# Row transfers released from the transposition, a first input loaded in halves, a convolution moved: one Trainium2 kernel of convolution, Fourier transform and MLP

## The chip, the core and the metric

The kernel runs on one core of a Trainium2 chip. The core has five instruction streams that run side by side and meet at semaphores: TensorE (PE; its weight loads are shown apart as PEld), VectorE (DVE), ScalarE (ACT), GpSimd (POOL) and SyncE (SP), which here only issues DMA transfers. The 16 DMA engines move data between DRAM and the on-chip memory. The metric is the device time of one execution in microseconds (us); less is better. A program's framework (a tile scheduler) puts the instructions of each stream in an order when the kernel is built, and adds the semaphore waits; on the chip each stream runs in that order and waits where it must.

## What is computed

Input `x` is (8, 4224, 192): eight batches of 4224 tokens. First a convolution along the tokens with seven taps per head, the taps a softmax of the weights; then the real part of a 2-D Fourier transform over tokens and channels is added; then a layer norm and an MLP (192 to 768 to 192, ReLU), with a residual.

```python
w = np.exp(weight - np.max(weight, axis=-1, keepdims=True))
w = w / (np.sum(w, axis=-1, keepdims=True) + 1e-09)
x_pad = np.concatenate([np.zeros((B, K - 1, D)), x], axis=1)
x_unf = x_pad[:, idx, :].reshape(B, S, K, H, D // H)
x = np.einsum('hk,bskhg->bshg', w, x_unf).reshape(B, S, D)
...
X = np.fft.fft(np.fft.fft(x, axis=1), axis=2)
u = x + np.real(X)
un = (u - mean(u)) / np.sqrt(var(u) + 1e-06)
out = u + np.maximum(un @ w_ch1, 0.0) @ w_ch2
```

## The kernel before

**Stages of a batch.** (1) *Convolution* (`conv_unit`, L397): windows `xt` of the input meet a banded matrix on PE (L417, PSUM tile `pc`), ACT or DVE evict them into `xa` (L423, L426), ACT sums their squares (L367), and `store_rows` (L372) writes the rows into a scratch `sc` in DRAM. (2) *Load and split*: the rows come back as `xs` with the token index as 33a + 128b (a on the partitions, 33 values of b in eight pieces), and `split_x` (L517) makes two fp16 parts, XH on ACT (L527) and XL on DVE (L528). (3) `stage_a` (L534): the transform over a, 16 tiles `pa`, evicted into the halves `yh` and `yl` (L553, L554). It reads all b at once, so it needs all eight pieces. (4) `stage_b` (L559): the transform over b and part of the channels, PSUM tile `pb`, evicted into V (L580, L582). (5) For each of the nine steps of a batch: `load_res` (L597) brings the convolved rows of that step from the scratch into the tile `u`; `prep` (L645) does the last transform on PE (L669, PSUM tile `pq`), adds it to `u` on DVE (L686, "the sums"), takes mean and variance (L693, L694), normalises on POOL into `un` and splits into `hl` (L722 to L739); `transposes` (L749) turns `hl` into `kt` by a DMA transposition on SP's queue; `mlp_hidden` (L767, PSUM tile `ph`) makes `hh` on ACT and its low part `hlo` on DVE (L786, L787); `mlp_out` (L791, PSUM tile `po`) adds its result into `u` (L813) and stores `u` (L821).

**Rows of a step.** `u` has four groups of rows. Groups 0 and 2 come by ordinary transfers on SP's queue (two or three each, L612); groups 1 and 3 by one indirect DMA each, which POOL issues (L618). There are eight `u` tiles; a step uses the tile that the step eight before it has left, so its transfers wait until that step's output store has landed.

**Order.** The loop at L997 runs over the 72 steps. At step n it places the MLP of step n, `prep` of steps n+2 and n+3, the transposition of step n+2, the rows of step n+4, and the stages 1 to 4 of later batches. `tc.issue_after(x)` makes the scheduler issue an instruction behind x. Before, the ordinary row transfers of all but the first four steps were so held behind `turn[0]`, the transposition that was placed last; the indirect ones behind `lows`, the last POOL instruction of `hl` two or three steps earlier. SP's transfers use eight semaphores in turn: one is issued only when the eighth before it has landed.

**The start.** Batch 0's convolution runs first, without cover. `load_first_x` (L491) loads its scratch back in 16 transfers: four ranges of b by four ranges of a, sorted by the last row that each reads. The ranges with b under 17 go to a tile in the space of `yh`, the others to one in that of `yl` (they read `xs_yh` and `xs_yl` in the profile). From L976 on, written by hand: the second transform's first tile, the convolution of the second batch in chunks (`conv_chunk`, L969; its matmuls held behind `staged["pe"]`), and the first `prep`, `sums` being its four pieces up to the norm's factor and `rest` the last two.

Of the kernel before, what the change touches and what calls it, by code (L numbers as in the profile page):

```python
# [34 lines left out]
AC = 32  # L35
# [91 lines left out]
def kernel(  # L127
# [363 lines left out]
    def load_first_x(bt):  # L491

        halves = [
            sb.tile([NA, 17, D], F32, tag=tag, name=f"xs_0_{tag}", bufs=1)
            for tag in ("yh", "yl")
        ]

        def rows_of(b0, b1):
            h, o = (halves[0], 0) if b0 < 17 else (halves[1], 17)
            return h[:, b0 - o : b1 - o]  # L500

        loads = []
        for b0, b1 in ((0, 9), (9, 17), (17, 25), (25, 33)):
            for ch in range(NA // AC):
                r = 33 * AC * ch + 128 * b0 - (S if b0 >= WRAP[ch] else 0)
                loads.append((r + 33 * (AC - 1) + 128 * (b1 - 1 - b0), r, ch, b0, b1))
        for _, r, ch, b0, b1 in sorted(loads):
            src = bass.AP(
                bt.sc.tensor, bt.sc.offset + r * D,
                [[33 * D, AC], [128 * D, b1 - b0], [1, D]],  # L510
            )
            load = nc.sync.dma_start(rows_of(b0, b1)[AC * ch : AC * (ch + 1)], src)
        for i, piece in enumerate(PIECES):
            bt.xs[i] = rows_of(*piece)
        return load.ins
# [43 lines left out]
    def stage_b(bt, it):  # L559
# [3 lines left out]
        for h in range(CG // CT):  # L563
            pb = ps.tile([128, CT, 2 * NM], F32, tag="f", name=f"pb_{b}_{it}_{h}", bufs=4)
            for i in range(CT):
                c = it * CG + h * CT + i

                parts = ((0, 2, NM),) if c else ((0, 1, NM), (1, 2, 0))
                for e0, e1, at in parts:
                    for n, (y, l) in enumerate(((bt.yh, 0), (bt.yh, 1), (bt.yl, 0))):  # L570
                        mm = nc.tensor.matmul(  # L571
                            pb[NJ * e0 : NJ * e1, i],
                            y[:NBD, c, e0:e1].rearrange("p e j -> p (e j)"),
                            R[:, l, at : at + 2 * NM],
                            start=(n == 0), stop=(n == 2),
                        )
# [7 lines left out]
                )  # L584

        if b + it == 0:
            staged.update(pe=mm.ins, act=up.ins)
        if it == 0:
            bt.V0 = sb.tile([128, 2, 6, 64], F16, tag="V0", name=f"V0_{b}")
        nc.gpsimd.tensor_copy(  # L590
# [6 lines left out]
    def load_res(bt, it, g):  # L597
# [6 lines left out]
        def fetch(part, first, *dims):  # L604
            src = bass.AP(
                bt.sc.tensor,
                bt.sc.offset + first * D,
                [[step * D, n] for step, n in dims] + [[1, D]],
            )
            late = turn[0] if b * NIT + it > 3 else None  # L610
            with tc.issue_after(late) if late else ExitStack():
                nc.sync.dma_start(part, src)  # L612

        if it == Q0 or g % 2:
            col = 0 if it == Q0 else 1 + 4 * it + g
            k = b * NIT + it
            with after(lows.get(k - 2, lows.get(k - 3))):
                nc.gpsimd.indirect_dma_start(  # L618
                    to, None, bt.sc[:S],
                    bass.IndirectOffsetOnAxis(ap=rows_sb[:, col : col + 1], axis=0),  # L620
                )
            return
# [22 lines left out]
    def prep(bt, it):  # L645
# [16 lines left out]
        for at, t in rows:  # L662
            for k3 in range(ND):

                po = pq[at, k3, 0] if it == Q0 else pq[at, k3]
                for r in range(2):
                    for n, (v, l) in enumerate(((0, 0), (0, 1), (1, 0))):
                        rhs = G[:, l, r, k3, t]
                        nc.tensor.matmul(  # L669
                            po, weights(v, ND * r + k3),  # L670
                            rhs[:, 0] if it == Q0 else rhs,
                            start=(r + n == 0), stop=(r == 1 and n == 2),
                        )

        uf = u.rearrange("p g (c k) -> p g c k", k=ND)
        pt = pq.rearrange("p k t c -> p t c k")
        if it == Q0:
# [296 lines left out]
            )  # L974

    stage_b(first, 0)  # L976
    conv_chunk(0)
    for f in sums(0) + rest(0):
        f()
    transposes(first, 0)  # L980
    conv_chunk(1)
# [110 lines left out]
```

## Time and profile before

| | us |
|---|---|
| median of three runs | 1274.29 (1269.73 to 1274.59) |
| the profiled execution | 1266.11 |
| its span, first to last instruction | 1264.1 |
| TensorE busy in it | 1175.6 (93%) |
| VectorE, GpSimd, ScalarE busy | 819.6, 769.2, 599.8 |
| DMA moved | 170.47 MB, mean 135 GB/s |

All rows shown below are of that profiled execution, in us from the start of its span. A row of the timeline has start, length, engine (SPq: SP's queue), line, operation and tiles written and read, a count, and in brackets how long the engine stood before it and what ended that. A busy TensorE is not TensorE at its peak, since the ends of its matmuls are modelled.

### The profile page before, as it was taken

What the parts mean: (1) busy time and instruction counts of PE and PEld (TensorE: products, weight loads), DVE (VectorE), ACT (ScalarE), POOL (GpSimd) and SP (SyncE); (2) the same over time, 40 slices, a digit from 0 to 9 for tenths busy, and PEclk for the clock granted to TensorE, in tenths of its full rate; (3) what the DMA queues carried; (4) which work ended last, traced back from release to release, by engine and by line L of the source; (5) the groups of instructions that cost most, each with busy time, mean ns of one, the idle gap of its engine ahead of it and who ended that gap; (6) DMA issues with size and microseconds to landing.
All of it is one profiled execution on the core that took longest, in us unless ns stands there. A gap on an engine that the chain in (4) does not pass through costs nothing.

```text
span 1264.1 us, 30150 instructions
## 1 busy us (share of the span) xinstructions
PE 1175.6 (93%) x12224; PEld 931.5 (74%) x12224; DVE 819.6 (65%) x1871; ACT 599.8 (47%) x983; POOL 769.2 (61%) x1103
## 2 busy tenths in 40 slices
PE   4089889998999999999899999999899999999998
PEld 4078667786778777887677867778677877777766
DVE  6666485677646865476655876467965687566543
ACT  4556564365444555446444554446444454332222
POOL 0206776577646777468564786557774778757760
PEclk9589999999999999999999999999999999999999
DMA  8933784558554675477654677555754444322331
GB/s 300 264 103 102 223 204 121 134 137 156 130 121 122 174 153 143 93 166 173 113 135 115 136 178 142 126 128 129 181 120 114 121 126 96 79 61 67 94 73 41
DMA packets 238506, 170.47 MB, mean 135 GB/s; under 512 B 119512, under 2 KB 222112, under 8 KB 238368
## 3 DMA queue, kind: packets, MB, share of 16 engines
q1 hardware_dynamic: 193912, 130.75, 43.3%
q10 hardware_dynamic: 37928, 24.44, 7.4%
q0 software_dynamic: 6528, 13.38, 4.5%
q8 instruction: 95, 1.56, 0.5%
q14 instruction: 43, 0.35, 0.1%
HBM read 83.82 MB, written 58.55 MB: 113 GB/s over the span
## 4 chain that ended last, share of the span: by engine, by line
PE 64%; DVE 10%; POOL 8%; DMA 8%; issue 3%; SPq 3%; ACT 2%; ACTq 0%; DVEq 0%; POOLq 0%
PE ph L782 24%; PE po L801 8%; PE po L807 8%; PE po L804 8%; DMA u<-sc 4%; PE pc L417 4%; PE pb L571 4%; PE pa L545 4%; PE pq L669 4%; POOL hl L739 2%; DVE u L686 2%; POOL u L618 2%; POOL y L714 2%; POOL un L722 2%; DVE hlo L787 2%
## 5 line engine op out<-in xcount | busy, mean ns | idle before, releaser
L782 PE MATMUL ph<-kt,W 128*128 128x512 f16 (+1 forms) x2160 | 493.0, 361 | 18.7 <-DVE hlo L787 17.5
L786 ACT ACTIVATE hh<-ph 128x512 f16<-128x512 f32 (+1 forms) x400 | 236.9, 592 | 443.9 <-PE ph L782 412.5
L787 DVE SCALAR_TENSOR_TENSOR hlo<-ph,hh 128x512 f16<-128x512 f32 (+1 forms) x400 | 270.9, 679 | 269.7 <-ACT hh L786 261.6
L801 PE MATMUL po<-W,hh 128*128 128x192 f16 x1584 | 386.3, 247 | 3.6 <-DVE u L813 2.8
L807 PE MATMUL po<-W,hlo 128*128 128x192 f16 x1584 | 387.0, 247 | 1.5 <-DVE hlo L787 1.5
L804 PE MATMUL po<-W,hh 128*128 128x192 f16 x1584 | 386.2, 247 | 0.0
L782 PEld LDWEIGHTS <-W 128*128 128x128 f16 x2160 | 192.1, 97 | 161.5 <-issue 16.0
L722 POOL TENSOR_SCALAR un<-u,mv,y 128x192 f32<-128x192 f32 x260 | 268.8, 1039 | 7.9
L618 POOL DMA_INDIRECT u<-sc,rows_sb x136 | 152.4, 1121 | 67.7 <-DMA xs_yl<-sc 36.8
L807 PEld LDWEIGHTS <-hlo 128*128 128x128 f16 x1584 | 155.2, 98 | 23.6 <-DVE hlo L787 1.9
L801 PEld LDWEIGHTS <-hh 128*128 128x128 f16 x1584 | 155.6, 98 | 19.4 <-ACT hh L786 1.6
L804 PEld LDWEIGHTS <-hh 128*128 128x128 f16 x1584 | 155.2, 98 | 17.6 <-issue 3.4
L686 DVE SCALAR_TENSOR_TENSOR u<-pq,g,u 128x128 f32<-128x128 f32 (+1 forms) x328 | 104.8, 379 | 69.5 <-DMA u<-sc 52.9
L545 PE MATMUL pa<-c_sb,XH 128*128 128x128 f16 x1024 | 101.4, 222 | 32.3 <-DMA xt<-in_xw_dram 24.9
L417 PE MATMUL pc<-xt,band 128*120 128x144 f32 x724 | 114.8, 297 | 15.0 <-DMA band<-line_d 11.0
L713 POOL TENSOR_SCALAR v<-mv 128x4 f32<-128x4 f32 (+1 forms) x71 | 17.1, 241 | 177.6 <-DVE mv L694 154.1
L739 POOL TENSOR_TENSOR hl<-un,hl 128x512 f16<-128x512 f32 (+2 forms) x142 | 119.5, 862 | 3.5
L590 POOL COPY V<-V 128x96 f16<-128x96 f16 x64 | 16.4, 260 | 172.9 <-DVE V L582 171.5
L417 PEld LDWEIGHTS pc<-xt,band 128*120 128x120 f32 x724 | 100.5, 189 | 23.5 <-issue 10.9
L545 PEld LDWEIGHTS <-XH 128*128 128x128 f16 x1024 | 81.9, 98 | 42.7 <-ACT XH L527 26.4
L553 ACT ACTIVATE yh<-pa 99x512 f16<-99x512 f32 x128 | 76.2, 597 | 77.5 <-PE pa L545 71.7
L528 DVE SCALAR_TENSOR_TENSOR XL<-xs,s_x,XH 128x768 f16<-128x768 f32 (+1 forms) x56 | 92.5, 1653 | 17.3 <-ACT XH L527 17.2
(132 smaller groups left out, 1570.4 us busy)
## 6 DMA issues: line engine op xcount, KB each, us to landing
out_dram<-u SPq DMA_DIRECT2D x64, 384.0 KB
xt<-in_xw_dram SPq DMA_DIRECT2D x40, 576.0 KB
sc<-xa ACTq DMA_DIRECT2D x30, 540.0 KB
xs<-sc SPq DMA_DIRECT2D x28, 288.0 KB
u<-sc SPq DMA_DIRECT2D x72, 96.0 KB
sc<-xa SPq DMA_DIRECT2D x12, 540.0 KB
xs<-sc SPq DMA_DIRECT2D x28, 192.0 KB
xs<-sc SPq DMA_DIRECT2D x7, 480.0 KB
```

The costliest lines, as they stand in the source:

```text
L417: nc.tensor.matmul(pc[:WR, h - h0], band[:, h, :WR], xt[:, :, h * GRP : (h + 1) * GRP], start=True, stop=True,)
L545: nc.tensor.matmul(pa[:, i], x[:, at], F[:, l], start=(n == 0), stop=(n == 2))
L618: nc.gpsimd.indirect_dma_start(to, None, bt.sc[:S], bass.IndirectOffsetOnAxis(ap=rows_sb[:, col : col + 1], axis=0),)
L686: nc.vector.scalar_tensor_tensor(to, src, bt.g, to, op0=ALU.mult, op1=ALU.add)
L722: (nc.vector if b + it == 0 else nc.gpsimd).tensor_scalar(un[:, g], u[:, g], mv[:, g, 0:1], y[:, g : g + 1], op0=ALU.subtract, op1=ALU.mult,)
L739: lower = (nc.vector if b + it == 0 else nc.gpsimd).tensor_tensor(bl[:, :, o : o + n], un[:, :ng, f], hi[:, :, f], op=ALU.subtract)
L782: nc.tensor.matmul(ph[:, n], W1[:, w, ht * 128 : (ht + 1) * 128], kt[:, k], start=(i == 0), stop=(i == len(order) - 1),)
L786: anchor[0] = nc.scalar.activation(hh, ph, AF.Relu).ins
L787: nc.vector.scalar_tensor_tensor(hlo, ph, 0.0, hh, op0=ALU.max, op1=ALU.subtract)
L801: nc.tensor.matmul(po[:, g % 2], hh[:, ht, tk], W2[:, ht, 0], start=(ht == 0), stop=False)
L804: nc.tensor.matmul(po[:, g % 2], hh[:, ht, tk], W2[:, ht, 1], start=False, stop=False)
L807: nc.tensor.matmul(po[:, g % 2], hlo[:, ht, tk], W2[:, ht, 0], start=False, stop=(ht == 5),)
```

## The change

Three parts. The row transfers (L612) are no longer held behind a transposition, and the indirect ones (L618) are held behind `lows` in the first batch alone. The first input's sixteen loads are sorted by half of b first (those under 17, then the others). And `sums(0)`, the first `prep` up to its norm, is written ahead of the second batch's first convolution chunk, whose matmuls are now held behind the last matmul of the first sums instead of the second transform's first tile.

```diff
@@ load_first_x
-                loads.append((r + 33 * (AC - 1) + 128 * (b1 - 1 - b0), r, ch, b0, b1))
-        for _, r, ch, b0, b1 in sorted(loads):
+                last = r + 33 * (AC - 1) + 128 * (b1 - 1 - b0)
+                loads.append((b0 >= 17, last, r, ch, b0, b1))
+        for _, _, r, ch, b0, b1 in sorted(loads):
@@ stage_b
-            staged.update(pe=mm.ins, act=up.ins)
+            staged.update(act=up.ins)
@@ load_res
-            late = turn[0] if b * NIT + it > 3 else None
-            with tc.issue_after(late) if late else ExitStack():
-                nc.sync.dma_start(part, src)
+            nc.sync.dma_start(part, src)
...
-            with after(lows.get(k - 2, lows.get(k - 3))):
+            with after(lows.get(k - 2, lows.get(k - 3)) if k < NIT else None):
@@ prep
+        staged.setdefault("pe", mm.ins)
@@ the start
     stage_b(first, 0)
+    for f in sums(0):
+        f()
     conv_chunk(0)
-    for f in sums(0) + rest(0):
+    for f in rest(0):
         f()
```

What the scheduler makes of it, at three places. First, SP's queue at the sixteen loads of the first input, before (xs_yh is the half with b under 17; 32x8 or 32x9 are rows of a by values of b):

```order
L512 DMA xs_yl<-sc_130 32x8x192 x2
L512 DMA xs_yh<-sc_130 32x8x192
L512 DMA xs_yh<-sc_130 32x9x192
L512 DMA xs_yl<-sc_130 32x8x192 x2
L512 DMA xs_yh<-sc_130 32x8x192
L512 DMA xs_yh<-sc_130 32x9x192
L512 DMA xs_yl<-sc_130 32x8x192 x2
L512 DMA xs_yh<-sc_130 32x8x192
L512 DMA xs_yh<-sc_130 32x9x192
```

(two of `xs_yl` and two of `xs_yh` follow once more), and in the change:

```order
L513 DMA xs_yh<-sc_130 32x8x192
L513 DMA xs_yh<-sc_130 32x9x192
L513 DMA xs_yl<-sc_130 32x8x192 x2
L513 DMA xs_yh<-sc_130 32x8x192
L513 DMA xs_yh<-sc_130 32x9x192
L513 DMA xs_yl<-sc_130 32x8x192
L513 DMA xs_yh<-sc_130 32x8x192
L513 DMA xs_yh<-sc_130 32x9x192
L513 DMA xs_yh<-sc_130 32x8x192
L513 DMA xs_yh<-sc_130 32x9x192
L513 DMA xs_yl<-sc_130 32x8x192 x5
```

The eight loads of `xs_yh` are now among the first eleven, where they were spread over all sixteen. On ACT and DVE the pieces of `xs_yh` are split first, where those of `xs_yl` were; the first two pieces that ACT takes are those of the 32x8 loads.

Second, PE at the first sums. Before, behind the second transform's first tile (pc is the second batch's convolution, pq the sums' PSUM tile, V_0 the weights of its matmuls):

```order
L417 MATMUL pc_0_0_697<-xt_0_632,band 120x144 x3
L417 MATMUL pc_0_3_702<-xt_0_632,band 120x144 x3
L417 MATMUL pc_0_6_707<-xt_0_632,band 120x144 x2
L417 MATMUL pc_1_0_771<-xt_1_634,band 120x144 x3
L669 LDWEIGHTS V_0_659
L669 MATMUL pq_0_716<-c_sb,V_0_659 128x130
```

and in the change:

```order
L668 LDWEIGHTS V_0_659
L668 MATMUL pq_0_695<-c_sb,V_0_659 128x130
L417 MATMUL pc_0_0_740<-xt_0_632,band 120x144 x3
L417 MATMUL pc_0_3_745<-xt_0_632,band 120x144 x3
L417 MATMUL pc_0_6_750<-xt_0_632,band 120x144 x2
L417 MATMUL pc_1_0_771<-xt_1_634,band 120x144 x3
```

All eighteen `pq` matmuls are now ahead of the convolution. Behind the first two of them, which need V's high half alone, 24 matmuls of the second transform's next tile stand, where six stood before.

Third, SP's queue in the third batch's third and fourth step (u_4 is the tile of that batch's step 4, counted from 0; kt_2 the transposition of step 2; xs and xt are inputs of the next two batches; out_dram an output store), before:

```order
L753 DMA_TRANSPOSE kt_2_5847<-hl_2_5766 128x12x128
L612 DMA u_4_5770<-sc_1462 80x1x192
L612 DMA u_4_5770<-sc_1462 48x1x192
L354 DMA xt_1_5903<-in_xw_dram 128x1152
L612 DMA u_5_5975<-sc_1462 128x1x192
L487 DMA xs_7_6012<-sc_3781 32x4x192
L487 DMA xs_7_6012<-sc_3781 96x4x192
L821 DMA out_dram<-u_0_4763 128x768
L753 DMA_TRANSPOSE kt_3_6034<-hl_3_5971 128x12x128
L612 DMA u_5_5975<-sc_1462 96x1x192
L612 DMA u_5_5975<-sc_1462 32x1x192
```

and in the change:

```order
L611 DMA u_6_6197<-sc_1462 128x1x192
L611 DMA u_6_6197<-sc_1462 112x1x192
L611 DMA u_6_6197<-sc_1462 16x1x192
L611 DMA u_7_6439<-sc_1462 128x1x192 x2
L487 DMA xs_6_5977<-sc_3781 32x4x192
L487 DMA xs_6_5977<-sc_3781 96x4x192
L487 DMA xs_7_6012<-sc_3781 32x4x192
L487 DMA xs_7_6012<-sc_3781 96x4x192
L753 DMA_TRANSPOSE kt_2_5847<-hl_2_5766 128x12x128
L354 DMA xt_1_5903<-in_xw_dram 128x1152
L821 DMA out_dram<-u_0_4763 128x768
L753 DMA_TRANSPOSE kt_3_6034<-hl_3_5971 128x12x128
```

The rows of steps 4 and 5 stood behind the transpositions of steps 2 and 3; now those of steps 6 and 7 stand ahead of the transposition of step 2, and so do both `xs` loads. POOL's indirect transfers move by as much. At the start, likewise, the eleven transfers for the first batch's steps 4 to 7 stand ahead of the second batch's first store and of the first transposition, directly behind seven for steps 0, 2 and 3. On DVE the parts of a step's sums, which stood apart where a part of the rows came later, now stand together; the number of evictions and splits between them is the same.

More of the change, by code (lines that the diff above doesn't have):

```diff
@@ L570, in stage_b @@
                     for n, (y, l) in enumerate(((bt.yh, 0), (bt.yh, 1), (bt.yl, 0))):
-                        mm = nc.tensor.matmul(
+                        nc.tensor.matmul(
                             pb[NJ * e0 : NJ * e1, i],
@@ L668, in prep @@
                         rhs = G[:, l, r, k3, t]
-                        nc.tensor.matmul(
+                        mm = nc.tensor.matmul(
                             po, weights(v, ND * r + k3),
```

## The prediction

> **What bounds the kernel now.** I read the page first, for the span and the slices, then the busy time by stretches, then who waited for whom on the two engines that matter, TensorE (PE) and VectorE (DVE), and last the timeline at the places the change touches.
>
> ```profile
> span 1264.1 us, 30150 instructions
> PE   4089889998999999999899999999899999999998
> ```
>
> Each digit is a slice of 31.6 us. TensorE is full except in the first slices, the second of them empty, so the matmuls set the time, and time can be won only where TensorE stands. There are two such places. The first is the start, here by stretches of 20 us (busy time of PE, PE's weight loads, DVE, ACT, POOL; then granted clock, DMA share, GB/s):
>
> ```profile
> 40.00:60.00 20.00, 0.00 (x0) 0.00 (x0) 9.10 (x8) 10.21 (x9) 4.04 (x5) 0.50 1.10 251
> 140.00:160.00 20.00, 15.42 (x131) 11.54 (x131) 11.75 (x21) 13.95 (x19) 16.30 (x18) 1.00 0.90 258
> ```
>
> From 40 to 60 us nothing runs on PE while the DMA engines are full: the first batch's convolved rows come back from DRAM. From 140 to 160 us PE lacks 4.6 us. The second place is the steady part, where each batch takes nine steps:
>
> ```profile
> 200.00:250.00 50.00, 50.00 (x516) 38.99 (x515) 26.45 (x67) 20.79 (x41) 27.46 (x47) 1.00 0.58 139
> 250.00:300.00 50.00, 47.59 (x513) 38.09 (x511) 37.56 (x79) 29.00 (x40) 38.39 (x51) 1.00 0.66 159
> ...
> 1000.00:1050.00 50.00, 49.85 (x533) 39.00 (x531) 40.16 (x90) 26.60 (x35) 40.59 (x55) 1.00 0.44 112
> ```
>
> Most stretches are full; one or two in each batch lack 2 us and more. The waits of PE and of DVE from 200 us to the end (total, times, longest) say why:
>
> ```profile
> PE ph L782 <- DVE hlo L787: 16.4, 21, 2.3
> PE pa L545 <- DVE u L686: 4.6, 3, 1.8
> ```
>
> ```profile
> DVE u L686 <- DMA u<-sc: 46.0, 15, 5.7
> ```
>
> PE stands 21.0 us because DVE is late with the low half of the hidden layer or stands itself at the sums of L686; and DVE stands 46.0 us in 15 places because the rows `u`, which SP fetches from the scratch, are not there. That is the wait the change aims at. One such place, first SP's issues, then DVE:
>
> ```profile
> 278.03 2.02 SPq L753 DMA_TRANSPOSE kt<-hl  x1
> 280.10 1.62 SPq L612 DMA_DIRECT2D u<-sc  x2
> ```
>
> ```profile
> 283.80 1.24 DVE L686 SCALAR_TENSOR_TENSOR u<-pq,g,u 128x192 f32<-128x192 f32 x4 [3.73 <-DMA u<-sc]
> ```
>
> The two row transfers start the moment the transposition in front of them is issued, and DVE, idle for 3.73 us, goes on 2 us after them. DVE executes in order, so the next eviction of the hidden layer waits too.
>
> **The change part by part.**
>
> *The split input of the first transform.* The first stage needs all of XH and XL, so all eight pieces must be split (ACT, then DVE) before PE starts. SP's rows, then ACT, DVE and PE:
>
> ```profile
> 46.05 0.38 SPq L954 DMA_DIRECT2D taps<-line_d  x1
> 48.41 2.90 SPq L354 DMA_DIRECT2D xt<-in_xw_dram  x2
> ```
>
> ```profile
> 53.35 0.87 SPq L612 DMA_DIRECT2D u<-sc  x1
> ```
>
> ```profile
> 50.83 6.11 ACT L527 ACTIVATE XH<-xs_yl,s_x 128x768 f16<-128x768 f32 x4 [9.79 <-DMA xs_yl<-sc]
> 56.84 6.55 ACT L527 ACTIVATE XH<-xs_yh,s_x 128x768 f16<-128x768 f32 x4
> 63.42 1.85 DVE L528 SCALAR_TENSOR_TENSOR XL<-xs_yh,s_x,XH 128x960 f16<-128x960 f32 x1 [0.30 <-ACT XH L527]
> 65.33 0.29 PE L545 MATMUL pa<-c_sb,XL 128*128 128x128 f16 x1 [0.85 <-DVE XL L528]
> ```
>
> SP issues a transfer only when the eighth before it has landed, so its issues tell landings. Counting the 16 loads as 1 to 16, `taps` is number 18 and waits for load 10 (landed by 46.05 at the latest), `xt` is 19 (load 11 by 48.41), the third row transfer is 23 (load 15 by 53.35). Now: the first `yl` pieces need load 13, and ACT starts at 50.83. Changed: the order shows all eight loads of the half `yh` among the first eleven, and the two pieces that ACT takes first need only numbers 1, 5, 8, 10. So ACT starts at 46.1, the four `yh` pieces (6.55 us) end at 52.7, with load 11 in time for the third. The `yl` pieces then wait for load 15 until 53.4, and end 6.1 us later at 59.5. DVE follows with the last piece, which is now a `yl` one of 1.5 us in place of the 1.85 us: 61.1. PE passes its wait at 61.2 in place of 65.33: **4.1 us**. The bounds: 2.4 us, if load 11 counts for all four pieces (48.41 against 50.83), and 4.7 us (46.1 against 50.83). Matmuls and bytes stay the same.
>
> What the clock does to this stage:
>
> ```profile
> 66.00:68.00 2.00, 2.00 (x22) 2.00 (x20) 0.69 (x1) 0.91 (x2) 0.00 (x0) 0.50 0.96 238
> ...
> 70.00:72.00 2.00, 2.00 (x39) 2.00 (x37) 2.00 (x4) 1.75 (x4) 0.00 (x0) 1.00 0.17 49
> ```
>
> After the idle stretch PE runs at 0.50 for some 5 us; a tile of twelve matmuls takes 1.1 us there and 0.6 us later, where DVE (about 0.7 us a tile) is the slower. Earlier or later release therefore moves the stage's end by some 0.4 us per us. [...]
>
> *The second batch's convolution behind the first sums.* The chain of waits and DVE:
>
> ```profile
> 78.75 1.30 PE pb L571 x23
> 80.05 2.75 PE pc L417 x22
> ...
> 83.19 0.92 PE pq L669 x16
> ```
>
> ```profile
> 80.17 1.07 DVE L582 SCALAR_TENSOR_TENSOR V<-pb,V 128x408 f16<-128x408 f32 x2 [1.48 <-ACT V L580]
> ```
>
> The sixteen `pq` matmuls need DVE's V, done at 81.24, but stand behind convolution matmuls until 83.19. In the changed order 24 matmuls of the second transform's next tile stand there, 1.1 us, which end before 81.24. The sums start 83.19 - 81.24 = **1.9 us** earlier, and with them the first normalisation and transposition. The moved convolution runs while DVE and ACT normalise, where PE stood anyway. Bounds: nothing, if ACT's evictions of the moved chunk come before the square root that it also does for the norm, and 2.75 us.
>
> *Row transfers not held.* At the start SP now issues eleven more transfers ahead of the second batch's first store and the first transposition:
>
> ```profile
> 63.90 6.58 SPq L612 DMA_DIRECT2D u<-sc  x7
> 82.54 1.15 SPq L381 DMA_DIRECT2D sc<-xa  x2
> ```
>
> Seven took 6.58 us, so eleven end 10.3 us after 70.5, at 80.8, and the store behind them, due 0.6 us earlier than now, at 81.9. It is hidden, with 1.1 us to spare; the transposition comes 3.6 us later still. If that cover goes, each us is lost in full.
>
> In the stretch from 140 to 160 us the row transfers for steps 4 and 5 came late:
>
> ```profile
> 138.35 0.97 DVE L686 SCALAR_TENSOR_TENSOR u<-pq,g,u 128x192 f32<-128x192 f32 x3 [5.04 <-DMA u<-sc]
> ```
>
> That stall goes. Of the 4.6 us that PE lacks behind it I take **3 us**, since the loads of the second batch's input (DMA share 0.90) stay. Bounds 0 and 4.6.
>
> In the steady part SP's order has the row transfers two steps ahead of now. All 15 stalls of DVE have the time of two steps (one is 150/9 = 17 us) to vanish. Of PE's 21.0 us I take three quarters, **16 us**, bounds 0 and 21. The stretch 1000:1050 speaks for that: DVE is busier there (40.2 of 50) than in 250:300 and PE lacks 0.15 us, so a crowded DVE without a stall costs next to nothing. I keep a quarter because four sums now stand together ahead of a split of 1.5 us and an eviction.
>
> On POOL and SP a transfer can now stand until an output store has landed that frees its tile. Behind it on SP are the next transposition and the `xs` loads, on POOL a normalisation. Cover: the program places transpositions more than a step before use, and in the whole run PE waited for one once (its waits from 100 to 200 us); `xs` loads lead too (SP, then ACT):
>
> ```profile
> PE ph L782 <- DMA kt<-hl: 0.8, 1, 0.8
> ```
>
> ```profile
> 390.37 3.35 SPq L487 DMA_DIRECT2D xs<-sc  x6
> ```
>
> ```profile
> 406.99 1.66 ACT L527 ACTIVATE XH<-xs,s_x 128x768 f16<-128x768 f32 x1
> ```
>
> 13 us lie between. A store's landing lies between the last one of the kernel, issued at 1261.24 + 0.33 with the span over at 1264.1, so 2.5 us for 96 KB, and 8.0 us for 540 KB (the chain at 94.69):
>
> ```profile
> 1261.24 0.33 SPq L819 DMA_DIRECT2D out_dram<-u  x1
> ```
>
> ```profile
> 41.02 9.71 DMA xs_yl<-sc
> ...
> 94.69 8.01 DMA sc<-xa
> ```
>
> Both are under 13 us, so I take nothing; I lean to the low end, because the queue is less full there. [...]
>
> **Sum.** 4.1 + 1.9 + 3 + 16 = 25.0 us. The profiled execution took 1266.1 us (span 1264.1), which gives 1241. The median of the three runs shown is 1274.3, 8.2 us more; against it, **1249 us**.
>
> **The rivals.**
>
> *The crowd, not the queue.* In the batch's busy stretch DVE has eight splits between its evictions; if those cause PE's waits and the stall only orders them, the steady gain is 2 us and the start's 6: 1274.3 - 8 = 1266. For it: waits also follow the stalls by up to 9 us. Against it: 1000:1050, though there are no splits there, and 200:250. Chance 0.15.
>
> *The change doesn't bring its transfers earlier.* With DMA engines full from 28 to 68 us, the reordered loads could land as a block, and later transfers could stand on SP at the output stores as long as they stood behind transpositions. Then only the convolution's 1.9 us remain: 1272. Against it: SP's issues show single landings about a us apart. Chance 0.08.
>
> *The stall moves to POOL and SP and grows.* Gathers standing at output stores delay POOL's normalisation, so transpositions, so PE. It decides once a stand exceeds the step of 17 us by which a transposition leads. If it did at each batch, doubling today's 21.0 us of PE's waits, with the start's 6 us won: 1274.3 - 6 + 21 = 1289. Against it: the longest landing in the chain of waits is the 9.7 us of a first load (the row at 41.02), with the DMA engines full. Chance 0.05.
>
> **How the numbers follow.** My forecast has 0.72. All bounds at their best make 4.7 + 2.75 + 4.6 + 21 = 33 us, so 1241, and the runs of before are spread by 5 us, which gives 1236 at the low end; the high end, 1268, takes in the first rival and the case that only the start pays. The median can be told from no change at about 0.5%, 6.4 us. Faster by more than that: the forecast and most of the first rival, 0.83; within it 0.11; slower 0.06.
>
> **What would show it.** ACT's first XH piece reads `yh` and starts near 46; PE's long wait at L545 ends near 61; `pq` stands ahead of `pc`, near 77; DVE's 46.0 us at `u` fall under 10, PE's 16.4 at `hlo` to about 4; 250:300 shows PE at 49 or more. I am wrong if DVE's stalls go and PE's waits stay (first rival), or if POOL's waits at L617 and SP's at L611 appear and `ph` begins to wait for `kt`.

## The result, and the profile after

| | before | after |
|---|---|---|
| median of four runs each, us | 1272.01 (1269.30 to 1274.59) | 1255.49 (1254.92 to 1256.52) |
| ratio, with its 95% interval | 1 | **0.9871** (0.9843 to 0.9899) |
| the profiled execution (its span), us | 1266.11 (1264.1) | 1254.92 (1253.1) |

The change makes the kernel 16.5 us faster by the medians and 11.2 us by the two profiled executions. The times of before lie 5 us apart from run to run, so parts of a few us are read from the traces, and only sums of them from the times. Two runs, one of the kernel before and one of the kernel with the convolution alone, took 1618 and 2058 us at granted clocks of 0.72 and 0.56, and are left out of the ratios further down.

Up to the first sums the start came out nearly as forecast. The timeline of the changed kernel, first ACT at the split of the first input, then PE at the first transform and at the first sums (start, length, engine, line, operation, tiles, count, and in brackets the idle time before):

```profile
46.94 6.54 ACT L528 ACTIVATE XH<-xs_yh,s_x 128x768 f16<-128x768 f32 x4 [6.25 <-DMA xs_yh<-sc]
53.39 6.10 ACT L528 ACTIVATE XH<-xs_yl,s_x 128x768 f16<-128x768 f32 x4
...
61.18 0.29 PE L546 MATMUL pa<-c_sb,XL 128*128 128x128 f16 x1 [0.59 <-DVE XL L529]
...
77.53 1.07 PE L668 MATMUL pq<-c_sb,V 128*128 128x130 f16 x16
78.44 0.82 PE L417 MATMUL pc<-xt,band 128*120 128x144 f32 x5
...
99.46 0.81 PE L782 MATMUL ph<-kt,W 128*128 128x512 f16 x3 [2.75 <-DVE hlo L787]
```

ACT splits the half `yh` first and starts at 46.94, where it started at 50.83; PE passes its wait for XL at 61.18, where it was 65.33; and `pq` stands ahead of `pc`, at 77.5, where it was 83.0. The last row is new: PE waits 2.75 us in the first hidden layer, behind DVE's `hlo`. DVE says why:

```profile
98.72 0.69 DVE L787 SCALAR_TENSOR_TENSOR hlo<-ph,hh 128x512 f16<-128x512 f32 x1 [4.01 <-DMA sc<-xa]
```

The tile `hlo` of the first step takes the buffer in which a chunk of the second batch's convolution (`xa`) stood, and must wait until that chunk is stored. The chunk is later now relative to the sums. The other risk of the start, the eleven more row transfers on SP, stayed hidden as foreseen: they are issued by 78.9, and the store behind them goes out at 82.3.

In the steady part, the stretches shown before, now of the changed kernel (busy time of PE, PE's weight loads, DVE, ACT, POOL; granted clock, DMA share, GB/s):

```profile
140.00:160.00 20.00, 17.40 (x147) 13.08 (x146) 14.42 (x29) 11.66 (x16) 16.23 (x17) 1.00 1.06 244
200.00:250.00 50.00, 48.87 (x518) 38.55 (x517) 27.16 (x69) 20.09 (x38) 30.40 (x50) 1.00 0.54 138
250.00:300.00 50.00, 46.84 (x493) 37.52 (x491) 40.77 (x90) 30.05 (x40) 37.16 (x50) 1.00 0.64 156
```

From 140 to 160 us PE lacks 2.6 us in place of 4.6 (not quite the same work, since the changed kernel is some 2 to 5 us ahead there). But from 250 to 300 it is busy for 46.84 us, less than before (47.59). The waits of PE from 200 us to the end (total, times, longest) tell what has happened:

```profile
PE pc L417 <- DMA xt<-in_xw_dram: 10.7, 4, 3.2
PE pc L417 <- DMA xt<-in_xv_dram: 2.6, 1, 2.6
PE po L801 <- ACT hh L786: 2.3, 2, 1.9
PE ph L782 <- DVE hlo L787: 2.2, 3, 1.1
PE po L807 <- DVE hlo L787: 2.0, 1, 2.0
```

The 16.4 us behind DVE's `hlo` in the hidden layer are down to 2.2 (2.0 came up behind it in the output, L807), the 4.6 at the sums are gone, and DVE's 46.0 us at `u<-sc` don't appear any more. In their place stand 13.3 us in which the convolution's matmuls `pc` wait for the input windows `xt`; before, PE waited for no window behind 200 us. So a wait on one transfer was exchanged for a wait on another. One such place, POOL, SP and PE of the changed kernel:

```profile
268.18 1.11 POOL L617 DMA_INDIRECT u<-sc,rows_sb  x1 [0.18 <-issue]
...
272.10 0.95 POOL L617 DMA_INDIRECT u<-sc,rows_sb  x1 [0.30 <-issue]
...
275.45 2.94 POOL L739 TENSOR_TENSOR hl<-un,hl 128x512 f16<-128x512 f32 x2
```

```profile
273.99 5.71 SPq L487 DMA_DIRECT2D xs<-sc  x4
279.80 5.08 SPq L753 DMA_TRANSPOSE kt<-hl  x1
284.94 0.57 SPq L354 DMA_DIRECT2D xt<-in_xw_dram  x1
```

```profile
290.50 0.75 PE L417 MATMUL pc<-xt,band 128*120 128x144 f32 x4 [3.16 <-DMA xt<-in_xw_dram]
```

The window load is still held behind the transposition that was placed last (L353). Three things put that one off. POOL issues four gathers (two are shown) ahead of the `hl` that it reads, which is done at 278.4. Four `xs` loads stand ahead of it on SP, until 279.7, and so end last of the two. And its own issue takes 5.08 us, where it took 2.02 at this place before. `xt` follows at 284.94, and PE, which wants it at 287.3, gets it at 290.50. The same load in the kernel before:

```profile
281.77 0.45 SPq L354 DMA_DIRECT2D xt<-in_xw_dram  x1
```

### The profile page after: what moved, and what is told of

It reads as the page before. It is cut to its first block, busy times and chain, and to the rows that moved or that the text cites. A ratio compares the mean times of both kernels' runs of the same rounds, so it can differ in the third digit from the quotient of the medians.

```text
span 1253.1 us, 30187 instructions
## 1 busy us (share of the span) xinstructions
PE 1169.8 (93%) x12224; PEld 928.6 (74%) x12224; DVE 822.2 (66%) x1871; ACT 598.3 (48%) x983; POOL 776.2 (62%) x1103
## 4 chain that ended last, share of the span: by engine, by line
PE 75%; DVE 8%; DMA 6%; POOL 5%; ACT 2%; issue 2%; SPq 1%; ACTq 0%; DVEq 0%; POOLq 0%
PE ph L782 29%; PE po L801 9%; PE po L807 9%; PE po L804 9%; PE pa L546 6%; PE pc L417 5%; PE pb L572 5%; PE pq L668 5%; DMA xt<-in_xw_dram 2%; DVE XL L529 2%; DMA sc<-xa 1%; ACT XH L528 1%; POOL y L714 1%; DMA xs_yh<-sc 1%; POOL un L722 1%
## 5 line engine op out<-in xcount | busy, mean ns | idle before, releaser
L807 PE MATMUL po<-W,hlo 128*128 128x192 f16 x1584 | 385.3, 246 | 2.2 <-DVE hlo L787 2.2
L722 POOL TENSOR_SCALAR un<-u,mv,y 128x192 f32<-128x192 f32 x260 | 274.2, 1060 | 6.9 <-POOL y L718 0.2
L617 POOL DMA_INDIRECT u<-sc,rows_sb x136 | 143.2, 1053 | 153.0 <-DMA out_dram<-u 57.3
L807 PEld LDWEIGHTS <-hlo 128*128 128x128 f16 x1584 | 154.9, 98 | 24.8 <-DVE hlo L787 2.7
L417 PE MATMUL pc<-xt,band 128*120 128x144 f32 x724 | 111.4, 294 | 28.7 <-DMA xt<-in_xw_dram 13.0
L739 POOL TENSOR_TENSOR hl<-un,hl 128x512 f16<-128x512 f32 (+2 forms) x142 | 124.2, 895 | 2.6
L713 POOL TENSOR_SCALAR v<-mv 128x4 f32<-128x4 f32 (+1 forms) x71 | 20.2, 284 | 151.2 <-DVE mv L694 125.9
L686 DVE SCALAR_TENSOR_TENSOR u<-pq,g,u 128x128 f32<-128x128 f32 (+1 forms) x328 | 103.1, 379 | 14.5 <-PE pq L668 9.7
L813 DVE SCALAR_TENSOR_TENSOR u<-po,fo,u 128x384 f32<-128x384 f32 (+1 forms) x136 | 81.3, 598 | 38.0 <-PE po L807 38.0
```

Of the source, the lines that this page charges most:

```text
L417: nc.tensor.matmul(pc[:WR, h - h0], band[:, h, :WR], xt[:, :, h * GRP : (h + 1) * GRP], start=True, stop=True,)
L617: nc.gpsimd.indirect_dma_start(to, None, bt.sc[:S], bass.IndirectOffsetOnAxis(ap=rows_sb[:, col : col + 1], axis=0),)
L722: (nc.vector if b + it == 0 else nc.gpsimd).tensor_scalar(un[:, g], u[:, g], mv[:, g, 0:1], y[:, g : g + 1], op0=ALU.subtract, op1=ALU.mult,)
L739: lower = (nc.vector if b + it == 0 else nc.gpsimd).tensor_tensor(bl[:, :, o : o + n], un[:, :ng, f], hi[:, :, f], op=ALU.subtract)
L807: nc.tensor.matmul(po[:, g % 2], hlo[:, ht, tk], W2[:, ht, 0], start=False, stop=(ht == 5),)
```

## The experiments

The twelve kernels ran in three groups of four, each group on a chip of its own, and each was timed in five rounds beside runs of the kernel before on that chip; the ratio is to those runs. It is not exactly the quotient of the two medians that stand beside it; the two differ by up to 0.002. The ratio of the change itself is that of the table above, measured apart from these. In the table at the end of this part all twelve stand together. "First `ph`" is the first hidden-layer matmul of a step, by which two traces can be compared step by step.

**The parts of the change alone.** First the order of the first loads, put into the kernel before:

```diff
-                loads.append((r + ..., r, ch, b0, b1))
-        for _, r, ch, b0, b1 in sorted(loads):
+                last = r + ...
+                loads.append((b0 >= 17, last, r, ch, b0, b1))
+        for _, _, r, ch, b0, b1 in sorted(loads):
```

> The kernel before with the reordered first loads alone. Theory (the prediction's first term, and after's trace): TensorE passes its XL wait at 61.2 instead of 65.3 us, 4.1 us earlier, and nothing between there and the steady part takes it back, so the time falls from 1272 to 1268. Rival: the four us are lost again before the first hidden layers, because the first kt or the first hlo comes no sooner (a store of sc<-xa stands before it); then TensorE still passes at 61.2, the first ph gains less than 1 us and the time stays at 1271 to 1272.

Measured: 1262.31 against 1266.19 us, ratio 0.9967 (0.9943 to 0.9991), 3.9 us by the medians. PE in its trace:

```profile
61.78 0.29 PE L546 MATMUL pa<-c_sb,XL 128*128 128x128 f16 x1 [0.53 <-DVE XL L529]
```

That is 3.55 us earlier than before, and the first `ph` of the first step comes 4.8 us earlier, of the second 4.6. The gain is clear of the noise and isn't lost in the start; the rival falls.

Second, the convolution behind the first sums:

```diff
-    conv_chunk(0)
-    for f in sums(0) + rest(0):
+    for f in sums(0):
+        f()
+    conv_chunk(0)
+    for f in rest(0):
         f()
```

(with the change of `staged["pe"]` that goes with it)

> The kernel before with the second batch's convolution behind the first sums alone. Theory (the prediction's second term): the pq matmuls start 1.9 us earlier (81.3 instead of 83.2) and the time falls by 1.9 to 1270; the trace of after, where this part is 1.35 us, says 1270.6. Rival: the moved convolution makes hlo's first use wait for the store of its chunk (2.75 us of TensorE in after at 99.46), which eats the gain: 1272 to 1273.

Measured: ratio 1.0009 (0.9980 to 1.0038), no difference. PE at the sums in the kernel before, then in this one:

```profile
83.03 1.07 PE L669 MATMUL pq<-c_sb,V 128*128 128x130 f16 x16
```

```profile
82.00 1.07 PE L669 MATMUL pq<-c_sb,V 128*128 128x130 f16 x16
...
102.75 0.59 PE L783 MATMUL ph<-kt,W 128*128 128x512 f16 x2 [1.43 <-DVE hlo L788]
```

The sums start 1.0 us earlier and the first `ph` of the first step 2.4 us earlier, but then PE waits 1.43 us for `hlo`, and the first `ph` of the second step is 1.2 us later than before. The rival was right. The sums gain less than the 1.9 us of the prediction because the 24 matmuls now ahead of them end 0.6 us behind DVE's V and not before it (V is done at 81.37).

Third, the row transfers of SP and POOL released, and nothing else (the two edits in `load_res`):

> The kernel before with the row transfers of SP and POOL released alone. Prediction's terms: 3 + 16 = 19 us, 1253. Theory now: DVE's 46 us at u and TensorE's 21 us behind DVE go, but TensorE waits some 13 us for the windows xt, which are still held behind the transposition and stand behind the released rows: a net of 8 to 10 us, 1262 to 1264, with waits of pc for xt of 10 us or more in all. Rival: the new wait comes from the shifted start and not from the release; then no waits for xt here and 1254 or less.

Measured: 1252.85 against 1266.19 us, ratio 0.9901 (0.9864 to 0.9938), some 12.5 us. PE's waits from 200 us on:

```profile
PE pc L417 <- DMA xt<-in_xw_dram: 7.9, 4, 2.1
PE ph L780 <- DVE hlo L785: 3.0, 5, 1.1
PE po L799 <- ACT hh L784: 2.2, 1, 2.2
PE po L805 <- DVE hlo L785: 2.0, 1, 2.0
PE pc L417 <- DMA xt<-in_xv_dram: 1.4, 1, 1.4
```

The waits for `xt` are there without the new start: they come from the release itself. From the third step to the sixth the first `ph` goes from 1.9 us behind the kernel before to 2.2 us ahead, and stays there until the windows' first wait. It won more than the 8 to 10 us expected, and less than the 19 of the prediction.

**The wait for the windows.** The changed kernel, with the windows no longer held:

```diff
-        with tc.issue_after(turn[0]) if turn[0] else ExitStack():
+        with ExitStack():
             nc.sync.dma_start(xt, src[:, ch * WC : (ch + 1) * WC])
```

> The changed kernel with the window loads xt released as well (not held behind the last transposition). Theory: pc's 13.3 us of waits for xt go, and TensorE has nothing late behind them: 1255.5 - 13 = 1242 to 1244. Rival 1 (the crowd): at the same places DVE is late with hlo by itself, TensorE's waits move to hlo and only a third goes: 1250 to 1252. Rival 2: the windows issued earlier stand on SP until their buffer is free, and the transpositions and row transfers behind them come late: 1255 or more, with waits of ph for kt or of DVE for u.

Measured: ratio 0.9816 (0.9775 to 0.9857). Behind 200 us PE waits 5.6 us in all, for `xt` not at all; its first `ph` gains 26 us on the kernel before between the fifth step and the last, so the crowd on DVE takes back next to nothing. But the start loses. SP, then PE:

```profile
126.75 0.35 SPq L354 DMA_DIRECT2D xt<-in_xw_dram  x1
127.96 4.97 SPq L753 DMA_TRANSPOSE kt<-hl  x1
```

```profile
141.54 1.04 PE L782 MATMUL ph<-kt,W 128*128 128x512 f16 x2 [5.78 <-DMA kt<-hl]
158.73 1.03 PE L782 MATMUL ph<-kt,W 128*128 128x512 f16 x2 [2.42 <-DMA kt<-hl]
```

A window of the third batch now stands ahead of a transposition that PE needs soon, while the DMA engines are full (a share of 1.10 from 130 to 134 us). So a part of the second rival came true, with windows issued too early in place of windows that stand. The next kernel keeps the hold for that one batch:

```diff
-        with tc.issue_after(turn[0]) if turn[0] else ExitStack():
+        with tc.issue_after(turn[0]) if turn[0] and b == 2 else ExitStack():
```

> The changed kernel with the window loads released from the fourth batch on, and still held for the third, whose loads stood ahead of the second batch's start in the run before (TensorE waited 8.2 us for kt at 141.5 and 158.7 us there). Theory: the 13 us of waits for xt from 290 us on go and the 8 us at kt don't come, so 7 to 8 us less than with all windows released: ratio to before about 0.975, some 16 us faster than the changed kernel. Rival: the early loads were not what held kt up, and the 8 us come back: ratio 0.981 to 0.982, as with all released.

Measured: 1238.21 against 1270.07 us, ratio 0.9760 (0.9727 to 0.9794), the fastest of all, some 14 us below the changed kernel. These are all of PE's waits from 200 us on in its trace:

```profile
PE ph L782 <- DVE hlo L787: 2.5, 3, 1.6
PE po L807 <- DVE hlo L787: 2.3, 1, 2.3
PE po L801 <- ACT hh L786: 0.7, 1, 0.7
```

So the 13.3 us were the windows' hold, and releasing it gives them back: from the seventh step to the last the first `ph` gains 23.4 us on the kernel before, where it gains 7.1 in the changed kernel. The waits for `kt` in the start, 8.2 us in two places, are gone too.

**SP's rows or POOL's gathers.** The kernel before with one of the two released:

```diff
 # SP alone
-            late = turn[0] if b * NIT + it > 3 else None
-            with tc.issue_after(late) if late else ExitStack():
-                nc.sync.dma_start(part, src)
+            nc.sync.dma_start(part, src)
 # POOL alone
-            with after(lows.get(k - 2, lows.get(k - 3))):
+            with after(lows.get(k - 2, lows.get(k - 3)) if k < NIT else None):
```

> The kernel before with SP's row transfers released, POOL's gathers as before. Theory: SP's transfers standing behind the transposition were the whole of DVE's 46 us at u, so DVE's waits there fall below 5 us and the ratio is that of both released, 0.990. Rival: the gathers, held behind the normalisation two or three steps earlier, come last as soon as SP's rows are in time; then DVE still waits 15 us or more for u and at most half of the gain is there, 0.995.

> The kernel before with POOL's gathers released, SP's row transfers held as before. Theory: DVE's waits at u stay at 40 us or more and the time doesn't change (0.998 to 1.002). Rival 1: the gathers carry a part, DVE's waits fall by 10 us or more and the ratio is 0.995 to 0.997. Rival 2: POOL stands at output stores and normalises later without anything gained: 1.005 and waits of ph for kt.

Neither expectation foresaw what came. SP alone made the kernel **slower**, 1281.88 against 1270.07 us, ratio 1.0105 (1.0068 to 1.0143). POOL alone gave the whole gain of both, 0.9896 (0.9859 to 0.9932). DVE's waits at the sums, first with SP alone, then with POOL alone:

```profile
DVE u L684 <- DMA u<-sc,rows_sb: 46.5, 13, 7.4
```

```profile
DVE u L686 <- DMA u<-sc: 17.4, 15, 3.5
```

With SP's rows early, DVE waits as long as before, for the gathers (`u<-sc,rows_sb`). With the gathers early, 17.4 us stay of the 46.0. Both kinds of transfer of a step hung on the same POOL instruction, the low half of `hl` two steps earlier: the transposition waits for it and SP's last rows stood behind the transposition, and the gathers were held behind it by name. One place with SP alone, POOL, SP, then DVE:

```profile
291.16 1.06 POOL L616 DMA_INDIRECT u<-sc,rows_sb  x1 [0.15 <-issue]
292.53 0.95 POOL L616 DMA_INDIRECT u<-sc,rows_sb  x1 [0.30 <-issue]
```

```profile
291.03 5.22 SPq L751 DMA_TRANSPOSE kt<-hl  x1
```

```profile
301.88 0.90 DVE L684 SCALAR_TENSOR_TENSOR u<-pq,g,u 128x128 f32<-128x128 f32 x3 [6.66 <-DMA u<-sc,rows_sb]
```

The gathers are issued by 293.5, beside the transposition, and DVE goes on at 301.88. DVE stands longer there than at any place before (6.66 against 5.7 us at most), and PE behind it: 27.1 us for `hlo` behind 200 us, 5.7 at most, against 16.4 and 2.3. The longest of these stands cost more than themselves, since PE goes on at half its clock behind them (the column ahead of the last two is the granted clock):

```profile
306.00:308.00 2.00, 2.00 (x8) 0.93 (x7) 2.00 (x3) 0.29 (x1) 1.94 (x3) 0.50 0.00 0
```

Four stands of 5.0 to 5.7 us are each followed by such a stretch, which ends 4 to 6 us after PE goes on; in the kernel before, whose stands are 2.3 us at most, there is one stretch behind 200 us, half as long (3.4 us by the mean clocks, behind a stand of 2.32 us that ends at 886.64). So in the kernel before the two kinds of transfer ended so close together that the release of one leaves the other as the last.

With POOL alone released the rows still come late: at the place of the prediction, where DVE went on at 283.80, they let it go on at 286.48 (the whole kernel is 1.1 us later there). But DVE has other work until then, since the scheduler puts an eviction, a split and an output sum ahead of the sums, where before they stood right behind the eviction at 279.39:

```profile
282.41 0.69 DVE L787 SCALAR_TENSOR_TENSOR hlo<-ph,hh 128x512 f16<-128x512 f32 x1 [1.26 <-ACT hh L786]
283.93 1.57 DVE L528 SCALAR_TENSOR_TENSOR XL<-xs,s_x,XH 128x768 f16<-128x768 f32 x1 [0.83 <-ACT XH L527]
285.42 0.61 DVE L813 SCALAR_TENSOR_TENSOR u<-po,fo,u 128x384 f32<-128x384 f32 x1
286.48 1.24 DVE L686 SCALAR_TENSOR_TENSOR u<-pq,g,u 128x192 f32<-128x192 f32 x4 [0.45 <-DMA u<-sc]
```

Here the gain comes by the order on DVE as well as by the transfer, and these runs don't separate the two. That the gathers are what is left over when SP's rows are early can be tested: holding them one step earlier must do.

```diff
 # SP alone released, and
-            with after(lows.get(k - 2, lows.get(k - 3))):
+            with after(lows.get(k - 3, lows.get(k - 4))):
```

> The kernel before with SP's row transfers released and POOL's gathers still held, but behind the low half of the normalised rows one step earlier. Theory: the gathers were what DVE waited for, and one step of some 15 us is more than their longest landing in the run with SP's rows alone released (11.9 us), so DVE's 46.5 us at u fall below 5 and the ratio is about 0.990, as with both released. Rival: the release of SP's rows is harmful by itself (SP stands at output stores, 51.8 us), and only gathers without any hold make up for it: 1.000 or more with waits of TensorE for hlo of over 20 us.

Measured: 1241.87 against 1267.56 us, ratio 0.9790 (0.9754 to 0.9825). DVE waits for no row any more behind 200 us. The theory holds in its cause, and the kernel is faster than it said, and faster than with both released, though neither the start nor the windows were touched. PE waits 5.6 us from 200 us on, and for `xt` not at all. POOL and SP at the place shown above for the changed kernel:

```profile
273.10 1.79 POOL L737 TENSOR_TENSOR hl<-un,hl 128x512 f16<-128x512 f32 x2
```

```profile
274.92 1.72 SPq L751 DMA_TRANSPOSE kt<-hl  x1
276.68 0.74 SPq L354 DMA_DIRECT2D xt<-in_xw_dram  x1
277.47 3.81 SPq L487 DMA_DIRECT2D xs<-sc  x4
```

No gather stands between the normalisation and `hl`, so `hl` is done at 274.9 (278.4 in the changed kernel), the transposition goes out ahead of the four `xs` loads and not behind them, its issue takes 1.72 us, and the window goes out at 276.68 in place of 284.94. As long as the windows are held, a hold of the gathers that is early enough is thus better than none: it keeps the gathers of later steps of the same batch out of the way, and with them the wait of POOL at output stores, of which there is none here behind 200 us. In the changed kernel it is:

```profile
POOL u L617 <- DMA out_dram<-u: 57.3, 15, 8.4
```

With the windows released from the fourth batch on there is nothing left to choose in the steady part: from the seventh step to the last the first `ph` gains 22.7 us here and 23.4 us there.

**The shared buffer at the start, and the convolution undone.** The first two chunks of the second batch's convolution in the buffers of `hlo`, the next two in those of `xa`:

```diff
-                second, ch, part, (("xa", 2), ("hlo", 2), ("xa", 2))[ch // 2],
+                second, ch, part, (("hlo", 2), ("xa", 2), ("xa", 2))[ch // 2],
```

> The changed kernel with the second batch's first two convolution chunks in the hlo buffers and its third and fourth in xa (swapped), so that the first hlo waits for stores of sc<-xa that went out earlier. Theory: TensorE's 2.75 us at 99.46 us behind DVE's hlo go, and the time falls by 2 to 3 us against the changed kernel (ratio to before 0.985). Rival: the wait moves on to the last two chunks, which now wait for the later stores to free xa, or the start's gain is lost at the first kt anyway: no change, 0.987.

Measured: 0.9854 (0.9819 to 0.9889). PE's 2.75 us at `hlo` are gone and the second step starts 4.3 us earlier than before, where it was 2.1. Then PE waits 2.8 us for a `kt` at 149 us, 0.8 in the changed kernel. The interval takes in both theory and rival.

> The changed kernel with the window loads released from the fourth batch on and the buffers of the second batch's convolution swapped, both together. Theory: the two gains lie at different places and add, 14 us and 2 us against the changed kernel: ratio to before 0.974. Rival: the first steps' gain is lost again at the next transposition (the swap alone showed 3.0 us at kt): 0.976, as without the swap.

With the windows released as well the ratio is 0.9768 (0.9731 to 0.9805): nothing beyond the 0.9760 without the swap. That is the rival's value; the theory's 0.974 lies in the interval too. Last, the changed kernel without its second part, with the windows held and released:

> The changed kernel without its second part: the second batch's convolution stands ahead of the first sums again. Theory: that part gives nothing in the end, since the first hlo then waits for the moved chunk's store; the ratio is the product of the two parts measured alone, 0.9967 x 0.9901 = 0.987, the same as with it. Rival: it is worth the prediction's 1.9 us, and without it the ratio is 0.9885; a second rival, that it costs 2 us, gives 0.9855.

> The changed kernel without its second part and with the window loads released from the fourth batch on. Theory: 0.976 as with the second part. Rival: without the shared hlo buffer's wait at the start (2.3 us of TensorE at 99.7) it is 2 us faster, 0.974, as with the buffers swapped.

Measured: 0.9932 (0.9903 to 0.9961) and 0.9787 (0.9752 to 0.9822). The first is 6 thousandths above the changed kernel, 7.7 us, and 6 above the product of its two parts alone; neither theory nor rivals said that. (The product of all three parts alone is 0.9877, which the change's interval takes in.) Its twelve runs lie 15.6 us apart (1253.44 to 1269.03). The profiled execution shows a pause that only some kernels have (columns as before, by stretches of 2 us):

```profile
198.00:200.00 2.00, 1.30 (x5) 0.31 (x4) 0.00 (x0) 0.41 (x2) 1.59 (x4) 1.00 0.22 62
200.00:202.00 2.00, 0.69 (x6) 0.39 (x5) 0.00 (x0) 0.37 (x1) 1.80 (x4) 1.00 0.19 49
...
204.00:206.00 2.00, 2.00 (x21) 1.75 (x20) 1.27 (x2) 1.09 (x3) 0.49 (x1) 0.50 0.97 342
```

PE stands 3.1 us of the 12 from 195 to 207, mostly with "issue" as its releaser, which is no wait that the profile shows, and then runs at half its clock (0.50) for 3.4 us by the mean clocks. Without the convolution but with the windows released it stands as long, with 6.8 us at half clock behind it; in the changed kernel 1.8 us, in that with both edits 2.0, in the others not at all. By the first `ph` of the seventh step against that of the sixth, the pause costs 5.0 and 6.4 us in the two kernels without the convolution, and 2.3 and 2.4 in the other two. At the last step the changed kernel is 6.5 us ahead of the one without the second part, by these two executions: 1.9 us of it are there at the sixth step, 2.7 are the pause, and 1.9 come behind it. Whether other executions of these kernels have the pause isn't known, since one of each was profiled. So what the second part is worth beside the others stays open: nothing alone, and up to the 7.7 us together, of which the pause is a part.

| kernel | ratio (95%) | PE's waits from 200 us, us | of them for `xt` | DVE at `u`, us |
|---|---|---|---|---|
| before | 1 | 23.0 | 0 | 47.2 |
| the change | 0.9871 (0.9843 to 0.9899) | 21.1 | 13.3 | 0 |
| first loads alone | 0.9967 (0.9943 to 0.9991) | 23.9 | 0 | 46.0 |
| convolution alone | 1.0009 (0.9980 to 1.0038) | 28.2 | 0 | 50.0 |
| rows alone | 0.9901 (0.9864 to 0.9938) | 16.5 | 9.3 | 0 |
| SP's rows alone | 1.0105 (1.0068 to 1.0143) | 28.9 | 0 | 46.5 |
| POOL's gathers alone | 0.9896 (0.9859 to 0.9932) | 13.2 | 0 | 17.4 |
| SP's rows, gathers a step earlier | 0.9790 (0.9754 to 0.9825) | 5.6 | 0 | 0 |
| change, windows released | 0.9816 (0.9775 to 0.9857) | 5.6 | 0 | 0 |
| change, windows from the fourth batch | 0.9760 (0.9727 to 0.9794) | 5.5 | 0 | 0 |
| change, buffers swapped | 0.9854 (0.9819 to 0.9889) | 14.5 | 9.6 | 0 |
| both of these | 0.9768 (0.9731 to 0.9805) | 11.8 | 0 | 0 |
| change without convolution | 0.9932 (0.9903 to 0.9961) | 20.4 | 12.3 | 0 |
| same, windows from the fourth batch | 0.9787 (0.9752 to 0.9822) | 10.5 | 0 | 0 |

(The last three columns are sums of the rows of the waits of one profiled execution each, DMA rows at `u` for DVE.)

## Why the prediction was right, and where it was not

The time lies in the range, and the gain is of the sign and kind foreseen: 1255.5 against 1249 forecast. It is smaller than forecast: 16.5 us by the medians and 11.2 by the two profiled executions, against 25.0. By the first `ph` in these two, 3.9 us had come at the seventh step, where the terms of the start foresaw 9.0, and 7.1 came behind it, where 16 were foreseen. By its steps:

*The split input, 4.1 us.* Right, by its own working: PE passes at 61.18 (61.2 foreseen), and alone the part is worth 3.9 us. That it fits to the tenth is luck: ACT starts at 46.94 and not at 46.1, and so ends its first half 0.8 us later, just when the prediction let the second half begin for another reason, a load (53.4).

*The convolution, 1.9 us.* Too high. The sums do start earlier, but by 1.0 us alone: the 24 matmuls ahead of them, priced at nothing because they "end before 81.24", end 0.6 us behind V. That the moved convolution "runs while DVE and ACT normalise" holds, but the moved chunk's store now ends after the first `hlo` wants the chunk's buffer: 2.75 us of PE in the changed kernel, 1.43 alone. Its bounds took in nothing, which is what it measured by itself; that is luck, since the reason given for that bound (ACT's square root) was another.

*The stretch from 140 to 160, 3 us.* Near: PE lacks 2.0 us less there, and with the rows alone the first `ph` gains 4.1 us from the third step to the sixth. In the changed kernel 2.3 us are lost again in the pause near 200 us.

*The steady part, 16 us.* The two steps of it that were argued from the profile held: DVE's 46.0 us at `u` went to nothing, and PE's waits behind DVE's `hlo` and `u` from 21.0 to 4.2 us (2.2 in the hidden layer, 2.0 in the output). So the release is worth more than three quarters of them, if nothing takes their place: from the seventh step to the last the first `ph` gains 23.4 us in the kernel with the windows released, and 22.7 with the gathers a step earlier. (The rows of PE's waits fall by 17.5 us; the rest is in matmuls that the profile shows shorter, and a busy PE is not PE at its peak.) In the changed kernel it gains 7.1. The step that failed is "Both are under 13 us, so I take nothing": it counted the next transposition and the `xs` loads as what stands behind the released transfers, priced those by their lead of 13 us, and left out the windows `xt`, which were still held behind the transposition, and which PE wants 2.4 us after their issue at the place shown. They cost 13.3 us of waits. The term was mis-sized twice, in opposite ways: the release was worth 23 us and not 16, and the cost behind it was not nothing, so that 7.1 us came of the 16. The 250:300 stretch, which was to show PE at 49 or more, shows 46.84.

*Which transfer.* The prediction read SP's row transfers as what DVE waited for, because the trace put the waits down to `u<-sc`, and named SP's order alone as the reason why all 15 stalls would go. Released alone they make the kernel slower, with 46.5 us of waits for the gathers. A releaser in the trace is the last of several; it doesn't say how close the next one is. The rows and gathers of one step hung on the same instruction, and that stood in the code. The forecast stood because the change releases both; by the reading alone, that was luck.

*The rivals.* The crowd on DVE fell: without the windows' hold PE waits 4.8 us behind DVE in the whole steady part. "Not earlier" fell with the 46.0 us. The rival on the slower side had the right mechanism and the wrong victim: POOL does stand at output stores (57.3 us), SP too (67.0 us at L611), and the gathers do put off `hl`, as the `xs` loads put off the transposition. But that didn't decide at 17 us, through `kt`, for which PE waits nowhere behind 200 us; it decided at the window behind the transposition, and took 13.3 us where 23 had been won.

## What to carry to other kernels

When several transfers feed one wait, list all of them and what each hangs on: a hold shared by two must be loosened for both, and loosening one can cost time (a ratio of 1.0105 here). When a hold is taken away, look for every other instruction that is still held behind the same thing, since it keeps its old place while the engine that needs it arrives earlier (13.3 us at the windows here). And a hold moved one step earlier may beat none while something else is still held (0.9790 against 0.9901 with the rows alone here), because it also keeps the early work out of the way.

## What the runs showed of the hardware

*The clock after an idle stretch.* PE starts the first transform at half its clock (0.50), and the time to full clock differs. The changed kernel starts it at 59.55, the kernel with the rows alone at 63.38; a stretch of each, in that order:

```profile
62.00:64.00 2.00, 2.00 (x23) 2.00 (x21) 0.69 (x1) 1.07 (x2) 0.00 (x0) 0.54 1.01 279
```

```profile
70.00:72.00 2.00, 2.00 (x28) 2.00 (x26) 1.04 (x3) 1.04 (x3) 0.00 (x0) 0.68 0.19 49
```

In stretches of half a us the clock of the changed kernel is 0.50 up to 63.5, 0.64 in the next and 1.00 from 64.0 on; that of the kernel before, which starts at 63.45, is 0.50 up to 68.0, then 0.58, and 1.00 from 68.5 on. Worked out as one such step from the mean clocks 0.54 and 0.68, and from 0.90 between 68 and 70 us in the kernel before, full speed came at 63.8 and 71.3, and at 68.4 before: 4.3, 7.9 and 5.0 us after the first matmul. With the rows alone the first transform ends 1.3 us later than before, though it starts at the same time (the first `pb` behind it at 79.33 against 78.02). Full speed comes 2.9 us later there, and at the 0.4 us per us that the prediction estimated this makes 1.2 of the 1.3 us. What sets the time to full clock isn't shown by these runs. The half-clock stretches behind the pause, 3.4 and 6.8 us, are worked out in the same way.

*The clock after a stand.* With SP's rows alone, PE falls to half clock behind each of its four stands of 5.0 to 5.7 us, for 6.8 us at the first of them by the mean clocks from 302 to 310 us (0.75, 0.50, 0.50, 0.55), and for as long at the other three.

*The landing of a gather.* Its median from issue to landing is 4.4 us with SP's rows alone released, the longest 11.9 us. At the place shown above, beside a transposition, DVE goes on 8.4 us after the second gather is issued (293.48 to 301.88).

*A pause without a wait.* The stand near 200 us, with "issue" as its releaser on PE, took 1.8 to 3.1 us of PE in four of the fourteen kernels and was followed by half clock in the two where it was longest. In three of the four ACT stands there too, 1.6 to 3.2 us ahead of an eviction of the convolution (L426), with "remote" as its releaser, a signal that the profile puts down to none of its instructions. The cause isn't shown by any run here.
